# A fused attention and two-MLP kernel: attention rounds taken two at a time, a new order of its first 36 turns, copies along their target, and an earlier start of the weight fold

## The chip, the cores and the metric

One core of a Trainium2 chip runs the whole program. The metric is device time in microseconds (us). TensorE (PE in the profile) does the products, ScalarE (ACT), VectorE (DVE) and GpSimd (POOL) work on the data between them, and SyncE (SP) issues all transfers from its one queue, in order.

## The reference

The weights arrive as float64, q, k and v as float32; the output is float32.

```
# attention: B=4, H=8, S=576, D=64; heads 0-3 "plain", heads 4-7 "dilated"
scores = q @ k.T / sqrt(D)
plain:   keep 0 <= i-j < 32
dilated: keep 0 <= i-j < 128 and (i-j) % 4 == 0
attn = softmax(scores);  x = attn @ v      # as tokens: x is 2304 x 512
# MLP 1: 512 -> 2048 -> 512
x = leaky(x @ w_in, 0.01) @ w_out
# MLP 2: 512 -> 1024 (two branches) -> 1024 -> 512
out = ((x @ w1) * (x @ w2)) @ w3 @ w_out2
```

## The kernel before

**Precision.** A float64 weight is turned to float32 on the chip (`to_float32`, L145: one scaling and two reads of the raw tile, L151 and L153 always on ScalarE, a shift and an add on VectorE, L157), then split into a high and a low part (`split_steps`, L108). Every product of the MLPs is three matmuls (`mm3`, L117, lines L120 to L122).

**Attention** goes in 32 rounds: a batch has four pairs of heads (two dilated, two plain), and each pair two rounds of five or four blocks of 64 queries. A round n is: the scores `ps_s` (L394: 16 or 20 small matmuls of 96 columns), scaling and mask (VectorE), the maximum, the exponentials (ScalarE, one for each block, L418), a normalization (POOL), the transposes `ps_p` with their copies to `pT` (ScalarE), the values `ps_o` (L472: 16 or 20 small matmuls of 64 columns), and two copies of the result into `x`, high part on ScalarE (L500), low part on VectorE (L503). For the first batch q and k are transposed by TensorE into `ps_qT` and `ps_kT`, and one copy each (L374, the engine by `TURN_ON`) writes `qT` or `kT` of 576 columns. Later batches are transposed on VectorE (`turn_halves`, L273 and L286). Scores, values, and the transposes of later rounds share two PSUM banks ("side").

**MLP 1** goes in turns. The tokens are cut into seven chunks (columns 320, 256, 320, 256, 384, 384, 384); turn (c, f) is chunk c with hidden block f of 16. `hidden_steps` makes 12 matmuls into `ps_h` and an activation `g` (ScalarE, L563), whose split parts feed the 12 matmuls of `project_steps` (`ps_x`) two turns later. `ps_h` has two PSUM banks, which the transposes `ps_w3T` share.

**Order.** Attention of batches 0 and 1, the conversion of the 32 MLP 1 weight tiles (`MLP_CONV` names their engines) and the first 36 turns stand in an order written out by hand: each letter of `START` is one step of one stage; `LOADS` is the order of its loads, and `RAW_AT` and `PAIR_AT` say in which buffers conversions work. After it the loop over turns runs; at each turn `pace` moves on the generator `attention(16, 32)` for batches 2 and 3. A `ps_s` or `ps_o` block thus stands as a block of small matmuls between the long matmuls of the MLP.

**Fold.** w3 @ w_out2 is computed on the chip. From turn `LATE` on, when attention is done, `begin_fold` sets up 12 conversions (8 tiles of w_out2, whose finished parts `wo2` are also written to memory, then 4 of w3, each turned by four transposes `ps_w3T`, L672), with two buffers for raw tiles, `rawf`. Each turn adds `FOLD_PACE` steps; a step is one conversion (`rf` is written by its two ScalarE reads), and once nine are made the products `ps_wp` too:

```
            conv3.step()
            if conv3.made < NI + 1:      # NI = 8
                return
            while w3T:
                ...
                wp_step()
```

**Last stretch.** In chunk 6, w1 and w2 are converted, and the fold's result comes back by `load_wp` and `split_wp`; then come the gate products `ps_ab` and the output `ps_y`.

Of the kernel before, what the change touches and what calls it, by code (L numbers as in the profile page):

```python
# [28 lines left out]
def tile_window_attention_two_mlps(  # L29
# [70 lines left out]
    def copy_on(e):  # L100
        return e.copy if e is nc.scalar else e.tensor_copy
# [134 lines left out]
    nat_t, v_t, qk_t = {}, {}, {}  # L236


    order, seq = [], []
    for b in range(B):  # L240
        plain = [b * HP + i for i in range(HP // 2)]
        dilated = [b * HP + i for i in range(HP // 2, HP)]
        seq += dilated + plain
        order += [(pi, r) for pi in dilated for r in range(2)]
        order += [(pi, r) for r in range(2) for pi in plain]

    def pair(pi):
        b, h0 = divmod(pi, HP)
# [108 lines left out]
    def turn_rows(m):  # L357
        pi, nm = seq[m // 2], "qk"[m % 2]
        plain = pair(pi)[2]
        c = 6 if plain else 8  # L360
        n = S // c
        t = nat_t.pop((nm, pi))
        ps = bank2(f"ps_{nm}T{pi}")
        for g in range(2):
            for c1 in range(c // 2):
                src = t[:n, g * (c // 2) + c1].rearrange("p j d -> p (j d)")
                nc.tensor.transpose(ps[:, g, c1 * n : (c1 + 1) * n], src, ident[:n, :n])
        yield
        dst = att.tile([P, S], F32, tag=nm + "T", name=f"{nm}T{pi}", bufs=2)
        if plain:  # L370
            to = dst.rearrange("d (p g c) -> d g c p", g=2, p=n)
        else:
            to = dst.rearrange("d (c p g) -> d g c p", g=2, p=n)
        copy_on(engine_of[TURN_ON[m]])(to, ps[:, :, : S // 2].rearrange("d g (c p) -> d g c p", p=n))  # L374
        qk_t[nm, pi] = dst
        yield

# [81 lines left out]
    def value_steps(n):  # L459

        pi, r = order[n]
        b, hp = divmod(pi, HP)
        t = pt.pop(n)
        nb = t.shape[1]
        ps = side_bank(f"ps_o{n}")[:, : nb * QB]
        b, hp = divmod(pi, HP)
        plain = pair(pi)[2]
        vt = v_t[4 * b + 2 * plain + r]
        h = 2 * (hp % (HP // 2))
        for i in range(nb):  # L470
            for j in range(2):
                nc.tensor.matmul(  # L472
                    ps[j * D : (j + 1) * D, i * QB : (i + 1) * QB],
                    vt[i][:, h + j, :],
                    t[:, i, j * QB : (j + 1) * QB],
                    start=True, stop=True,
                )
        yield
        x = xs[hp][:, :, b % 2 * S : (b % 2 + 1) * S]
        views = []  # L480
        s0, s1 = r * HS[0], r * HS[0] + nb * QB
        if plain:
            views.append((x[:, :, s0:s1], ps))
        else:
            spans = []
            for g in range(DILATION):
                j0, j1 = max(0, s0 - g * SR), min(SR, s1 - g * SR)
                if spans and spans[-1][2:] == (j0, j1):
                    spans[-1] = (spans[-1][0], spans[-1][1] + 1, j0, j1)
                elif j0 < j1:  # L490
                    spans.append((g, 1, j0, j1))
            x = x.rearrange("d i (j r) -> d i r j", r=DILATION)
            for g, m, j0, j1 in spans:
                src = bass.AP(
                    ps.tensor, ps.offset + g * SR + j0 - s0,
                    [list(ps.ap[0]), [SR, m], [1, j1 - j0]],
                )
                views.append((x[:, :, g : g + m, j0:j1], src))
# [12 lines left out]
    def attention(n0, n1):  # L511

        for m in range(n0, n0 + 4):
            transpose_qk(m)
            load_qk(m + 2)
            if m % 2:
                yield
        load_v(n0 // 2 + 1)
        scores(n0)
        yield  # L520
        scores(n0 + 1)
        normalize(n0)
        yield
        for n in range(n0, n1):
            run(turn_p(n))
            normalize(n + 1)
            yield
            if n % 8 != 3:
                scores(n + 2)
                yield  # L530
            transpose_qk(n + 4)
            load_qk(n + 6)
            yield
            if n % 8 == 3:
                scores(n + 2)
                yield
            run(value_steps(n))
            m = n // NA * 4
            if n % NA in (2, 3):
                load_v(m + n % NA)  # L540
            elif n % NA in (5, 7):
                load_v(m + 4 + (n % NA == 7))
            yield


# [221 lines left out]
    with ExitStack():  # L767
# [39 lines left out]
        RAW_AT = "WWWWWWWWWWWWWWWWWWWWWWWWNWNWNWNW"  # L807
        PAIR_AT = "KKVVKKVVKKVVKKVVKKVVKKVKVKVKVKVK"

        def raw_early(i):  # L810
            place, tag, bufs = homes[RAW_AT[i]]
# [8 lines left out]
        for f in range(NF + AHEAD):  # L820
# [13 lines left out]
        runs += [(c, 0, NF) for c in range(2, NCH)]  # L834
        turns = [(c, f, f0, f1) for c, f0, f1 in runs for f in range(f0, f1)]
        START = (
            "L~L~~~~LTL~Y~~LT~Y~~TSYLTMLSXYEMSLX~M~~RETXN~YL~PERTLNSYCL~RVMNPXxSCyELTMLPYLVCXTxRE"
            "yVNLYL~PLxRSLGCLyNAL~MVGBXPxDLSEyUSMA~D~R~CX~N~MBVGEXLGPD~U~C~~RDxNVIyAOPx~GC~y~BHDI"
            "ULAOIVGgOHBcxGLEylHUgDIRDANgcBOPcAGJLCUBDlIVLUAOxBlHyGULADIHgOBcAJGLUgADlBHcIlLUBOHI"
            "LUgGOHIDAGOIJDBGOALUgJADGgBcDlALHUIZBOHILczGBOJgDLAGlJBcDlALUgHBcUIlLUJILOgIUGJOIDGA"  # L840
            "HOBDGALHUgLADOIcBHGOALclBGJglBDUADHIUBcUIlJgUIOgIHcGOlAGDJgOADBOJGcUBlHIcGAlOAHDGBZg"
            "DBUHgDLAULIUBHOIUzGIOJADGIOBJDALUGLcOBJclIDAOglJGcUgAlDIHcBGOALDBHUgGIUADHOBlILUBJOI"
            "UgOIJcOF|JcLlFgHcLlSlgSMLXJMEFJcXlELHRcNlHgRFLPgNJCLPclJCFVSxcLlyHFSgMLXHMEXVFSxRgyJ"
            "NEMFPcHZClzXSgRENVMHXLxRENyHgPRHNCPJCJclgVclJxLgyPclJCVclVxyJxyHclHgHgHgJJclgJclZczl"
            "JJclSSMXMEXRENPRNCVxyPCVxyLLL"
        )
        LOADS = "0123a45b67cwwdwwwwwwwwwwwwwwwwwwwwwwwwwwwwww89ABefCDEFghGHi"
        def late_turn(i):
            turn_halves(2 * HP + i)
            yield  # L850
# [108 lines left out]
        for c, f0, f1 in runs:  # L959
# [28 lines left out]
            for f in range(f0, f1):  # L988
# [77 lines left out]
```

## Time and profile before

| | |
|---|---|
| three timed runs | 866.89, 867.5, 869.97 us; median 867.5 |
| profiled execution | 868.56 us |
| its span | 866.6 us (1.96 us lie outside it) |
| granted TensorE clock, mean | 0.998 |
| TensorE busy | 848.2 us, 98% |
| ScalarE, VectorE, GpSimd busy | 352.6, 346.7, 210.8 us |
| DMA | 103.58 MB |

All times that follow are of the profiled execution, counted from the start of its span. A window's row gives each engine's busy time within the stretch; a wait is the idle time of an engine ahead of an instruction, with what ended it; matmuls are pipelined, so a matmul's own duration is longer than the distance to the next one's start.

### The profile page before, as it was taken

The page shows a single profiled execution, that of the slowest core. Times are in us where ns is not written, and L with a number is a line of the kernel's source. Part 1 is how long each engine was busy: PE and PEld are TensorE (multiplying, and loading weights), DVE is VectorE, ACT ScalarE, POOL GpSimd, SP SyncE. Part 2 cuts the span into 40 slices and gives each one's busy share as a digit, 9 for nine tenths or more (in the row PEclk, how much of TensorE's full clock was granted, in tenths as well). Part 3 has the DMA queues.
Part 4 walks back from the last instruction along what each step waited for, and adds up shares of the span by engine and source line. Part 5 has one row for each costly group of instructions (what it writes and reads, how often), then busy time and mean ns, then how long its engine had stood idle before and what let it go on. Part 6 is the DMA issues. An engine that isn't in the chain of part 4 may idle for free.

```text
span 866.6 us, 14693 instructions
## 1 busy us (share of the span) xinstructions
PE 848.2 (98%) x5774; PEld 772.0 (89%) x5774; DVE 346.7 (40%) x704; ACT 352.6 (41%) x879; POOL 210.8 (24%) x236
## 2 busy tenths in 40 slices
PE   7999998999999999999999999999999999999998
PEld 7799997999999999989899999998888888888887
DVE  4999976344453432274434177731021011000000
ACT  4999945223443343364433175632131121111111
POOL 3311101122322232263222134223123112111110
PEclk9999999999999999999999999999999999999999
DMA  6976575183333311189887575341001000000001
GB/s 152 309 214 231 179 169 137 34 193 73 82 98 92 78 45 50 47 294 349 300 289 236 165 239 155 113 135 49 25 1 61 24 13 13 25 12 13 25 13 48
DMA packets 87333, 103.58 MB, mean 120 GB/s; under 512 B 42849, under 2 KB 65633, under 8 KB 87265
## 3 DMA queue, kind: packets, MB, share of 16 engines
q1 hardware_dynamic: 87264, 102.65, 39.0%
q8 instruction: 45, 0.74, 0.4%
q14 instruction: 24, 0.19, 0.1%
HBM read 85.72 MB, written 16.91 MB: 118 GB/s over the span
## 4 chain that ended last, share of the span: by engine, by line
PE 77%; DMA 7%; DVE 6%; ACT 5%; issue 4%; POOL 2%; SPq 0%; POOLq 0%; DVEq 0%; ACTq 0%
PE ps_ab L120 7%; PE ps_ab L122 7%; PE ps_ab L121 7%; PE ps_x L120 6%; PE ps_x L122 5%; PE ps_x L121 5%; PE ps_h L120 5%; PE ps_h L122 5%; PE ps_h L121 5%; PE ps_y L122 4%; PE ps_y L121 4%; PE ps_y L120 4%; PE ps_s L394 2%; PE ps_o L472 2%; PE ps_wp L122 2%
## 5 line engine op out<-in xcount | busy, mean ns | idle before, releaser
L120 PE MATMUL ps_h<-x,win 128*128 128x384 f32 (+2 forms) x448 | 142.5, 318 | 4.9 <-ACT g L563 4.2
L122 PE MATMUL ps_h<-x,win 128*128 128x384 f32 (+2 forms) x448 | 140.7, 314 | 0.0
L121 PE MATMUL ps_h<-x,win 128*128 128x384 f32 (+2 forms) x448 | 140.4, 313 | 0.0
L120 PE MATMUL ps_x<-gs,wout 128*128 128x384 f32 (+2 forms) x368 | 119.0, 325 | 0.0
L743 DVE TENSOR_TENSOR ab<-a,ps_ab 128x512 f32<-128x512 f32 (+1 forms) x40 | 25.2, 633 | 233.3 <-ACT a L741 225.8
L120 PE MATMUL ps_ab<-ys,w 128*128 128x512 f32 (+1 forms) x320 | 117.7, 368 | 0.6 <-DVE ab L743 0.6
L121 PE MATMUL ps_x<-gs,wout 128*128 128x384 f32 (+2 forms) x368 | 117.7, 320 | 0.1
L122 PE MATMUL ps_ab<-ys,w 128*128 128x512 f32 (+1 forms) x320 | 117.7, 368 | 0.0
L121 PE MATMUL ps_ab<-ys,w 128*128 128x512 f32 (+1 forms) x320 | 117.6, 368 | 0.0
L122 PE MATMUL ps_x<-gs,wout 128*128 128x384 f32 (+2 forms) x368 | 117.4, 319 | 0.0
L112 POOL TENSOR_TENSOR p<-ab,p 128x512 fp32r<-128x512 f32 (+1 forms) x40 | 47.0, 1177 | 211.3 <-ACT p L110 211.3
L110 DVE CAST gs<-g 128x384 fp32r<-128x384 f32 (+2 forms) x92 | 41.3, 449 | 128.9 <-ACT g L563 103.3
L120 PEld LDWEIGHTS ps_h<-x,win 128*128 128x128 f32 x448 | 84.8, 189 | 8.2 <-ACT g L563 6.1
L112 POOL TENSOR_TENSOR gs<-g,gs 128x384 fp32r<-128x384 f32 (+2 forms) x64 | 59.5, 929 | 133.5 <-DVE gs L110 133.5
L563 ACT ACTIVATE g<-ps_h 128x384 f32<-128x384 f32 (+2 forms) x112 | 49.1, 439 | 96.8 <-PE ps_h L122 80.2
L121 PEld LDWEIGHTS ps_h<-x,win 128*128 128x128 f32 x448 | 84.9, 190 | 0.3
L122 PEld LDWEIGHTS ps_h<-x,win 128*128 128x128 f32 x448 | 84.8, 189 | 0.4
L741 ACT COPY a<-ps_ab 128x512 f32<-128x512 f32 (+1 forms) x40 | 21.6, 543 | 139.5 <-PE ps_ab L122 139.5
L120 PEld LDWEIGHTS ps_x<-gs,wout 128*128 128x128 f32 x368 | 69.5, 189 | 1.7
L121 PEld LDWEIGHTS ps_x<-gs,wout 128*128 128x128 f32 x368 | 69.7, 189 | 1.3 <-POOL gs L112 0.4
L122 PEld LDWEIGHTS ps_x<-gs,wout 128*128 128x128 f32 x368 | 69.7, 189 | 0.6
L120 PEld LDWEIGHTS ps_ab<-ys,w 128*128 128x128 f32 x320 | 60.1, 188 | 11.1 <-DVE ab L743 1.0
(109 smaller groups left out, 1553.1 us busy)
## 6 DMA issues: line engine op xcount, KB each, us to landing
wo<-wo_dram SPq DMA_DIRECT2D x32, 512.0 KB
raw<-in_moe_w_in_dram SPq DMA_DIRECT2D x16, 512.0 KB
raw<-in_moe_w_out_dram SPq DMA_DIRECT2D x16, 512.0 KB
rawf<-in_moe_w_dram SPq DMA_DIRECT2D x16, 512.0 KB
raww<-in_moe_w_dram SPq DMA_DIRECT2D x16, 512.0 KB
q<-in_q_dram SPq DMA_DIRECT2D x48, 140.0 KB
k<-in_k_dram SPq DMA_DIRECT2D x48, 140.0 KB
v<-in_v_dram SPq DMA_DIRECT2D x60, 96.0 KB
```

The lines of the kernel that those rows point to most:

```text
L110: copy_on(e_hi)(hi, src)
L112: e_lo.tensor_tensor(lo, src, hi.bitcast(F32), op=ALU.subtract)
L120: nc.tensor.matmul(ps, a[1], b[0], start=first, stop=False)
L121: nc.tensor.matmul(ps, a[0], b[1], start=False, stop=False)
L122: nc.tensor.matmul(ps, a[0], b[0], start=False, stop=last)
L394: nc.tensor.matmul(ps[j * QB : (j + 1) * QB, i - bl.start], qt[d, i * QB : (i + 1) * QB], kt[d, first_key(i, plain) : first_key(i, plain) ...
L472: nc.tensor.matmul(ps[j * D : (j + 1) * D, i * QB : (i + 1) * QB], vt[i][:, h + j, :], t[:, i, j * QB : (j + 1) * QB], start=True, stop=True,)
L563: nc.scalar.activation(g, ps, AF.Prelu, alpha=SLOPE)
L741: nc.scalar.copy(t, ps[0][:, :n])
L743: nc.vector.tensor_tensor(g, t, ps[1][:, :n], op=ALU.mult)
```

## The change

Attention takes two rounds at a time: both transposes, both values, both scores, both normalizations. Its steps go from 68 to 36, and `pace` is set to match. In batch 3 the plain heads come first, and `v_seq` orders the loads of v to suit. `START` is a new order: five warm-up matmuls (`~`) fewer, batch 1's attention spread otherwise among the turns; with it go `LOADS`, `RAW_AT`, `PAIR_AT`, `MLP_CONV` (GpSimd 10, VectorE 13, ScalarE 9 of the first scalings, against 14, 11, 7) and `TURN_ON` (five of eight copies on ScalarE, against two). The copies of `qT`, `kT` and of the dilated heads' `x` run through their target in order and step through PSUM. The fold begins after turn (4, 11) instead of (4, 13), takes 1.4 and later 1.3 steps a turn instead of 1.35, and stops at nine conversions until turn (5, 3). `wpf` has two buffers.

```diff
-    TURN_ON = "DDAADDDD"
-    MLP_CONV = tuple(x + "AD" for x in "GGDGGDGGADADGDGGAGGDDADADGGGAADD")
+    TURN_ON = "AAADADAD"
+    MLP_CONV = tuple(x + "AD" for x in "GGDGDDGGADAADAADDGADAGGADDDDGAGD")
...
+        if b == B - 1:
+            rounds, pairs, v_order = rounds[::-1], pairs[::-1], v_order[2:] + v_order[:2]
...
-            to = dst.rearrange("d (p g c) -> d g c p", g=2, p=n)
+            to, dims = dst.rearrange("d (p g c) -> d p g c", g=2, p=n), "d g (c p) -> d p g c"
...
-            x = x.rearrange("d i (j r) -> d i r j", r=DILATION)
-            for g, m, j0, j1 in spans:
+            x = x.rearrange("d i (j r) -> d i j r", r=DILATION)
+            edges = sorted({0, s0 % SR, s1 % SR, SR})
+            for j0, j1 in zip(edges, edges[1:]):
+                g = [g for g in range(DILATION) if s0 <= g * SR + j0 and g * SR + j1 <= s1]
                 src = bass.AP(
-                    ps.tensor, ps.offset + g * SR + j0 - s0,
-                    [list(ps.ap[0]), [SR, m], [1, j1 - j0]],
+                    ps.tensor, ps.offset + g[0] * SR + j0 - s0,
+                    [list(ps.ap[0]), [1, j1 - j0], [SR, len(g)]],
                 )
...
-        for n in range(n0, n1):
+        for n in range(n0, n1, 2):
             run(turn_p(n))
-            normalize(n + 1)
             yield
-            if n % 8 != 3:
-                scores(n + 2)
-                yield
-            transpose_qk(n + 4)
-            load_qk(n + 6)
+            run(turn_p(n + 1))
...
-            run(value_steps(n))
+            for i in (n, n + 1):
+                run(value_steps(i))
...
+            for i in (n + 2, n + 3):
+                scores(i)
...
+            for i in (n + 2, n + 3):
+                normalize(i)
             yield
...
-        t = late.tile([P, DM], F32, tag="wpf", name=f"wpf{ib}", bufs=1)
+        t = late.tile([P, DM], F32, tag="wpf", name=f"wpf{ib}", bufs=2)
...
-        LATE = (4, 13)
-        FOLD_PACE = 1.35
+        LATE, HOLD = (4, 11), (5, 3)
+        FOLD_PACE = (1.4, 1.3)
...
-                    owed[0] += FOLD_PACE
-                    while owed[0] >= 1:
+                    held = (c, f) < HOLD
+                    owed[0] += FOLD_PACE[not held]
+                    while owed[0] >= 1 and not (held and conv3.made > NI):
                         owed[0] -= 1
                         fold_step()
```

**TensorE in the loop over turns, an attention block.** Before, the scores of a round (here round 24; `x10` is ten rows of two matmuls) stand alone among the products `ps_x` of turn (3, 7), and so do the values of round 22, some 25 rows later:

```order
L451 MATMUL ps_p22_1_3569<-ident_84,s22_3330 96x128
L394 MATMUL ps_s24_3606<-kT14_3506,qT14_3367 64x96 x10
L121 MATMUL ps_x3_0_0_3277<-gs_1654,wout7_1266 128x256
...
L122 MATMUL ps_h3_10_3639<-x3_79,win10_1272 128x256
L472 MATMUL ps_o22_3665<-pT22_3571,v11_3272 64x64 x8
L120 MATMUL ps_x3_0_0_3277<-gs_1654,wout8_1289 128x256
```

In the changed kernel two rounds' blocks follow each other at once, here the scores of rounds 20 and 21 within the hidden products of turn (3, 4), and their values ahead of the products of turn (3, 6):

```order
L121 MATMUL ps_h3_4_3338<-x2_78,win4_888 128x256
L400 MATMUL ps_s20_3164<-kT8_2842,qT8_2835 64x96 x10
L400 MATMUL ps_s21_3186<-kT9_3062,qT9_3055 64x96 x10
L122 MATMUL ps_h3_4_3338<-x2_78,win4_888 128x256
...
L122 MATMUL ps_h3_8_3572<-x3_79,win8_1233 128x256
L478 MATMUL ps_o20_3354<-pT20_3251,v10_3125 64x64 x10
L478 MATMUL ps_o21_3367<-pT21_3323,v10_3125 64x64 x10
L120 MATMUL ps_x3_0_0_3286<-gs_1921,wout6_1257 128x256
```

In this part of the program scores make seven such pairs and values eight; before, scores and values shared a block in three places, and stood alone in the others.

**TensorE at the first transposes of w3.** Before, they stand one by one among the products of turn (5, 2), and hidden products of turns (5, 3) and (5, 4) are ahead of them:

```order
L122 MATMUL ps_x5_0_1_4885<-gs_1654,wout1_860 128x384
L672 MATMUL ps_w3T0_4964<-ident_84,wf8_4914 128x128 x4
L121 MATMUL ps_x5_0_0_4884<-gs_1654,wout2_937 128x384
```

In the changed kernel the products of turns up to (5, 3) come first, and then three transposed tiles and twelve products of the fold stand in one run ahead of the hidden products of turn (5, 4) (of the twelve rows of `ps_wp` the first and the last are shown):

```order
L122 MATMUL ps_x5_0_1_4893<-gs_1921,wout3_1009 128x384
L684 MATMUL ps_w3T0_4931<-ident_84,wf8_4843 128x128 x4
L684 MATMUL ps_w3T1_4954<-ident_84,wf9_4922 128x128 x4
L120 MATMUL ps_wp0_0_4962<-wo2_0_0_4939,w3T0_4936 128x512
...
L122 MATMUL ps_wp0_1_4963<-wo2_1_1_4941,w3T0_4936 128x512
L684 MATMUL ps_w3T2_4989<-ident_84,wf10_4945 128x128 x4
L120 MATMUL ps_h5_4_5025<-x0_76,win4_888 128x384
```

Between the last value matmuls (`ps_o31`) and `ps_w3T0` there were 181 long matmuls, and there are now 114.

**ScalarE in the same place.** Before, an activation `g` stands every few rows between the reads `rf` of a raw tile (`rf8` is the ninth conversion):

```order
L151 ACTIVATE rf8_4915<-rawf8_4865 128x512
L153 ACTIVATE rf8_4915<-rawf8_4865 128x512
L634 COPY st_86<-ps_x4_0_1_4085 128x384
L110 CAST wo2_7_4923<-wf7_4871 128x512
L563 ACTIVATE g_85<-ps_h5_3_4898 128x384
L563 ACTIVATE g_85<-ps_h5_4_4939 128x384
L151 ACTIVATE rf9_4956<-rawf9_4878 128x512
```

In the changed kernel the reads for conversions 5 to 12 and their splits stand between two activations; the first and the last rows of that run are

```order
L575 ACTIVATE g_85<-ps_h5_3_4906 128x384
L110 CAST wo2_3_4716<-wf3_4666 128x512
L151 ACTIVATE rf4_4708<-rawf4_4632 128x512
...
L110 CAST w3T1_4959<-ps_w3T1_4954 128x512
L151 ACTIVATE rf10_4946<-rawf10_4850 128x512
L153 ACTIVATE rf10_4946<-rawf10_4850 128x512
L151 ACTIVATE rf11_4981<-rawf11_4929 128x512
L153 ACTIVATE rf11_4981<-rawf11_4929 128x512
L110 CAST w3T2_4994<-ps_w3T2_4989 128x512
L575 ACTIVATE g_85<-ps_h5_4_5025 128x384
```

On ScalarE the reads of the 12 conversions stood between the activations of turns (4, 13) and (5, 5); they now stand between those of (4, 15) and (5, 4), eight of the twelve behind that of (5, 3).

## Rows read from the trace of the kernel before

**Rows 1.** The profile page: the span, and TensorE (PE): busy time, share, instructions.

```profile
span 866.6 us, 14693 instructions
...
PE 848.2 (98%) x5774; PEld 772.0 (89%) x5774; DVE 346.7 (40%) x704; ACT 352.6 (41%) x879; POOL 210.8 (24%) x236
```

**Rows 2.** Windows of two stretches (columns: stretch, length, busy time by engine, clock, DMA, GB/s).

```profile
60.00:80.00 20.00, 20.00 (x158) 20.00 (x157) 18.35 (x41) 19.56 (x36) 5.29 (x5) 1.00 0.89 299
112.00:166.00 54.00, 50.46 (x526) 47.45 (x526) 33.20 (x83) 22.55 (x91) 5.62 (x6) 1.00 0.49 120
```

**Rows 3.** Waits of TensorE, 112 to 166 us: total, times, longest.

```profile
PE ps_s L394 <- DVE kT L286: 0.9, 1, 0.9
PE ps_s L394 <- DVE x L503: 0.8, 1, 0.8
PE ps_h L120 <- ACT g L563: 0.7, 1, 0.7
```

**Rows 4.** The chain that ended last, whole span: start, us, what.

```profile
6.51 1.38 PE warm L884 x6
...
156.90 1.32 PE ps_o L472 x40
177.81 1.47 PE ps_s L394 x32
```

**Rows 5.** The same chain within 320 to 332 us.

```profile
328.59 0.81 PE ps_s L394 x16
329.40 0.37 PE ps_h L120
...
330.30 0.73 PE ps_o L472 x20
```

**Rows 6.** Groups by form, ScalarE (ACT), 0 to 166 us: busy, mean ns, idle before.

```profile
L500 ACT CAST x<-ps_o 128x288 fp32r<-128x288 f32 x4 | 2.7, 673 | 4.2 <-PE ps_o L472 4.2
...
L500 ACT CAST x<-ps_o 128x320 fp32r<-128x320 f32 x4 | 1.7, 424 | 1.7 <-PE ps_o L472 1.7
...
L374 ACT COPY kT<-ps_kT 128x576 f32<-128x576 f32 x1 | 0.7, 697 | 0.9 <-PE ps_kT L367 0.9
```

**Rows 7.** Timeline of ScalarE in the fold: start, us, instruction [idle before <-releaser].

```profile
359.69 0.37 ACT L500 CAST x<-ps_o 128x256 fp32r<-128x256 f32 x1 [3.03 <-PE ps_o L472]
...
361.89 0.78 ACT L151 ACTIVATE rf<-rawf 128x512 f16<-128x512 f32 x1
...
389.02 0.80 ACT L151 ACTIVATE rf<-rawf 128x512 f16<-128x512 f32 x1 [2.06 <-DMA rawf<-in_moe_w_dram]
...
395.74 0.81 ACT L151 ACTIVATE rf<-rawf 128x512 f16<-128x512 f32 x1 [2.75 <-DMA rawf<-in_moe_w_dram]
...
398.49 0.81 ACT L151 ACTIVATE rf<-rawf 128x512 f16<-128x512 f32 x1 [0.88 <-DMA rawf<-in_moe_w_dram]
```

**Rows 8.** Timeline of TensorE in the same stretch.

```profile
359.31 0.34 PE L472 MATMUL ps_o<-pT,v 96*64 96x64 f32 x4
...
384.26 0.45 PE L120 MATMUL ps_h<-x,win 128*128 128x384 f32 x1 [2.05 <-ACT g L563]
...
385.51 0.52 PE L120 MATMUL ps_h<-x,win 128*128 128x384 f32 x1
385.83 0.52 PE L121 MATMUL ps_h<-x,win 128*128 128x384 f32 x1
...
395.01 0.60 PE L672 MATMUL ps_w3T<-ident,wf 128*128 128x128 f32 x4
```

**Rows 9.** Windows within the fold, columns as in Rows 2.

```profile
362.00:380.00 18.00, 18.00 (x106) 18.00 (x105) 13.00 (x18) 12.23 (x20) 11.00 (x12) 1.00 0.69 244
384.00:388.00 4.00, 3.73 (x14) 3.74 (x15) 3.86 (x7) 2.89 (x6) 2.75 (x3) 0.67 0.68 200
...
396.00:400.00 4.00, 3.88 (x23) 3.52 (x22) 2.70 (x4) 3.06 (x5) 3.37 (x4) 1.00 1.04 418
```

**Rows 10.** Waits of TensorE, 500 to 600 us.

```profile
PE ps_h L120 <- ACT g L563: 1.2, 3, 0.6
```

More of the change, by code (lines that the diff above doesn't have):

```diff
@@ L236, in tile_window_attention_two_mlps @@
     nat_t, v_t, qk_t = {}, {}, {}
-    order, seq = [], []
+    order, seq, v_seq = [], [], []
     for b in range(B):
@@ L242, in tile_window_attention_two_mlps @@
         dilated = [b * HP + i for i in range(HP // 2, HP)]
-        seq += dilated + plain
-        order += [(pi, r) for pi in dilated for r in range(2)]
-        order += [(pi, r) for r in range(2) for pi in plain]
+        rounds = [(pi, r) for pi in dilated for r in range(2)]
+        rounds = [rounds, [(pi, r) for r in range(2) for pi in plain]]
+        pairs, v_order = [dilated, plain], [4 * b, 4 * b + 1, 4 * b + 2, 4 * b + 3]
+        if b == B - 1:
+            rounds, pairs, v_order = rounds[::-1], pairs[::-1], v_order[2:] + v_order[:2]
+        order += rounds[0] + rounds[1]
+        seq += pairs[0] + pairs[1]
+        v_seq += v_order
     def pair(pi):
@@ L321, in load_v @@
             return
+        m = v_seq[m]
         b, plain, r = m // 4, m % 4 >= 2, m % 2
@@ L370, in turn_rows @@
         if plain:
-            to = dst.rearrange("d (p g c) -> d g c p", g=2, p=n)
+            to, dims = dst.rearrange("d (p g c) -> d p g c", g=2, p=n), "d g (c p) -> d p g c"
         else:
-            to = dst.rearrange("d (c p g) -> d g c p", g=2, p=n)
-        copy_on(engine_of[TURN_ON[m]])(to, ps[:, :, : S // 2].rearrange("d g (c p) -> d g c p", p=n))
+            to, dims = dst.rearrange("d (c p g) -> d c p g", g=2, p=n), "d g (c p) -> d c p g"
+        copy_on(engine_of[TURN_ON[m]])(to, ps[:, :, : S // 2].rearrange(dims, p=n))
         qk_t[nm, pi] = dst
@@ L484, in value_steps @@
         else:
[L485 to L491, printed above, removed]
-            x = x.rearrange("d i (j r) -> d i r j", r=DILATION)
-            for g, m, j0, j1 in spans:
+            x = x.rearrange("d i (j r) -> d i j r", r=DILATION)
+            edges = sorted({0, s0 % SR, s1 % SR, SR})
+            for j0, j1 in zip(edges, edges[1:]):
+                g = [g for g in range(DILATION) if s0 <= g * SR + j0 and g * SR + j1 <= s1]
                 src = bass.AP(
-                    ps.tensor, ps.offset + g * SR + j0 - s0,
-                    [list(ps.ap[0]), [SR, m], [1, j1 - j0]],
+                    ps.tensor, ps.offset + g[0] * SR + j0 - s0,
+                    [list(ps.ap[0]), [1, j1 - j0], [SR, len(g)]],
                 )
-                views.append((x[:, :, g : g + m, j0:j1], src))
+                views.append((x[:, :, j0:j1, g[0] : g[-1] + 1], src))
         for x, src in views:
@@ L518, in attention @@
         load_v(n0 // 2 + 1)
-        scores(n0)
+        for n in (n0, n0 + 1):
+            scores(n)
         yield
-        scores(n0 + 1)
-        normalize(n0)
+        for n in (n0, n0 + 1):
+            normalize(n)
         yield
-        for n in range(n0, n1):
+        for n in range(n0, n1, 2):
             run(turn_p(n))
-            normalize(n + 1)
             yield
-            if n % 8 != 3:
-                scores(n + 2)
-                yield
-            transpose_qk(n + 4)
-            load_qk(n + 6)
+            run(turn_p(n + 1))
+            turn = [lambda m=m: (transpose_qk(m), load_qk(m + 2)) for m in (n + 4, n + 5)]
+            last = n >= (B - 1) * NA
+            late = n % NA == (0 if last else 4)
+            if not late:
+                for f in turn:
+                    f()
             yield
-            if n % 8 == 3:
-                scores(n + 2)
-                yield
-            run(value_steps(n))
+            for i in (n, n + 1):
+                run(value_steps(i))
             m = n // NA * 4
[L539 to L542, printed above, removed]
+            if last and n % NA in (0, 2):
+                load_v(m + 2 + n % NA // 2)
+            elif n % NA == 2:
+                load_v(m + 2)
+                load_v(m + 3)
+            elif n % NA in (4, 6):
+                load_v(m + 2 + n % NA // 2)
+            yield
+            for i in (n + 2, n + 3):
+                scores(i)
+            if late:
+                for f in turn:
+                    f()
+            for i in (n + 2, n + 3):
+                normalize(i)
             yield
@@ L806, in tile_window_attention_two_mlps @@
         }
-        RAW_AT = "WWWWWWWWWWWWWWWWWWWWWWWWNWNWNWNW"
-        PAIR_AT = "KKVVKKVVKKVVKKVVKKVVKKVKVKVKVKVK"
+        RAW_AT = "WWWWWWWWWWWWWWWWWNWNWNWWNNWNWWWW"
+        PAIR_AT = "VVKVKVKNVKKVKKVKKVKKVKKVKKVKKVKK"
         def raw_early(i):
@@ L836, in tile_window_attention_two_mlps @@
         START = (
[L837 to L845, printed above, removed]
+            "L~L~~~~LTL~Y~~LT~Y~~SLTMXSYLETMXL~Y~~RESNTMLRPXYNSCLETMXPLYVLCRSENMTxXVYLRPxyNLETyL~"
+            "Y~G~CSRDALNPMLBVLXCLSUxLEPMLGyVXSDxR~CG~N~yIMVEOPXF~C~~xVAGy~x~RA~yNBHGADLUBDIULBLDO"
+            "IgUHEOLcGAlHGgRADNIDgOAPcBJGClLUALDIPcVClOxVByLHxUByIUBHOIUgGOHIFLgLAJLgDLBOGJcGDlAL"
+            "cDLlBHcUALlIUHBOIUGSOIDSAGOJgADFGgHBZLALcBUHgDIUzHlIMgOBJXGOEDJGcUAlHRgcNMIBXHlAUgOB"
+            "HDIGEUDJOIRGAOJBNAcUJGcDIlDAJlOgBcGHglLBULADLUIHcBOIlLgUJGOgDAGJIcDBlAOHZGBUzLHADLUg"
+            "IclBJOgUIGOJIcGADlBDJcAOUBGJIcLDAULOBPlILHUClIGOAHDgGBOADHUgGBcIULPAJOClgDIFLJBLOLJU"
+            "cIFVcGLlHOxADGyBlLSDgUASMIJcBXFEHULGIRDANJMgXBOEUPLHOIRlCNJgOcF|HlFHgclcSglSMXHMEXVV"
+            "gRxHLENyJgRxNyJclPZHCczlPgHCVgVxLyHxyPJCVclHxgyHJJclgHclgJJclgHclHgJJclgJclZczlJJclS"
+            "SMXMEXRENPRCNVxyPCVxyLLL"
         )
-        LOADS = "0123a45b67cwwdwwwwwwwwwwwwwwwwwwwwwwwwwwwwww89ABefCDEFghGHi"
+        LOADS = "0123a45b67wcww8wwwwwwwwdww9ewwwAwwwwwwwwwwwwwBCwwDEwFfghGHi"
         def late_turn(i):
@@ L949, in pace @@
         def pace(c):
-            owed[0] += 39 / 28 if c < LATE[0] else 2.25
+            owed[0] += 26 / 28 if c < LATE[0] else 10 / 6
             while owed[0] >= 1:
```

## The prediction

> **What bounds the kernel now.** I read the profile page first. TensorE is busy for 848.2 of 866.6 us [rows 1], so most of what the change can win lies in 18 us of idle time and in matmuls that take longer than they must. Two views then say where. The windows show a stretch near the start where TensorE has no gap while ScalarE (19.56 of 20) and VectorE (18.35) have nearly none either, and a later one, 112 to 166 us, where TensorE idles for 54.00 - 50.46 = 3.5 us, the largest of it for a `kT`, an `x` and a `g` [rows 2, 3]. From there to the end TensorE waits little; the one wait over 2 us stands inside the fold [rows 8]. The chain of waits shows what no idle time shows: a block of small attention matmuls costs the long matmuls around it something at its edge. The long matmul behind a `ps_s` block takes 0.37 us in the chain [rows 5], against 0.17 us where long ones follow each other (106 in 18.00 us, [rows 9]).
>
> **The change, part by part.** The sum is made against the profiled execution, 868.56 us (span 866.6 and 1.96 outside it); the median of three, 867.5, lies 1.06 below it.
>
> *Rounds in pairs, loop over turns.* Two `ps_s` blocks of 16 cost 2 x 0.81 = 1.62 us apart, and 1.47 together; two `ps_o` blocks of 20 cost 1.46 apart and 1.32 together [rows 4, 5]. With the slower matmul behind the block (0.37 - 0.17 = 0.20) a pairing saves 0.15 + 0.20 or 0.14 + 0.20, so about 0.35 us of TensorE. Seven pairs of scores and eight of values make 15 x 0.35 = 5.25; three places shared a block already and a part of their 0.2 is gone, less 0.6: **-4.65**, from -3.5 to -5.5. This time is TensorE's own and nothing covers it, unless a wait on one of the two side banks takes it back (the fourth rival).
>
> *START.* A series of six warm-up matmuls takes 1.38 us in the chain [rows 4], so five are 5 x 0.23 = 1.15: **-1.2**. The chain `ident`, masks, first load of q decides there, so this may be nothing. Batch 1's attention is brought forward and spread, so that its `kT`, `x` and `g` are wanted at other times: of the 3.5 us [rows 2, 3] I let one wait of 1.0 stay, **-2.5** (0 to -3.5). Four more pairings by the price above: **-1.4**. The early part, to about 60 us, I put at nothing, from -2 to +3: ScalarE gets three more copies of 0.70 us [rows 6] and two more first scalings of 0.8 us (priced as the read of a raw tile, [rows 7]), 3.7 us in all, in front of the stretch where it is full, and VectorE and GpSimd lose as many. Together **-5.1**, from +3 to -9.
>
> *Copies along the target.* ScalarE's copy of 288 columns into a strided target takes 673 ns, one of 320 columns into a plain one 424 [rows 6]. If the target was what costs, each falls by some 0.25 us, 1.0 us for four; if a strided read of PSUM costs as much, nothing is won. No row shows such a read. Either way these copies lie beside matmuls, and I count 0. [...]
>
> *Second `wpf` buffer, chunk 6.* TensorE waits there 1.2 us in three waits [rows 10], behind activations that stand after the splits of w1, w2 and the fold's result on ScalarE. A buffer frees only the part that waits for the transfer: **-0.9**, from 0 to -1.2.
>
> *Fold.* Here the order shows what the diff alone does not. Call T the time of the last value matmul. Before, T is 359.31, the first read of a raw tile starts 2.6 us later, the ninth, which `ps_w3T0` needs, at 389.02, and the eleventh, which `ps_w3T2` needs, at 398.49 [rows 7, 8]: 27.1 and 36.6 us after the first. TensorE reaches `ps_w3T0` at 395.01 without a wait [rows 8], because 181 long matmuls (30.8 us), a wait and a slow stretch lie between. Now 114 lie between, 114 x 0.17 = 19.4 us, and after 3.8 us more (two sets of transposes, twelve products of 512 columns) `ps_w3T2`, so TensorE asks for the eleventh conversion at T + 23.2. The order starts the conversions little earlier against T: two copies of `x` stand ahead of them, T + 1.3.
> How long eleven conversions take decides. *Upper end:* the pace of before, 36.6 us, and about 2.2 from the reading to the finished tile: T + 40.1, a wait of **16.9 us**. *Lower end:* the transfers in the queue up to the eleventh raw tile (raw tiles, finished parts written and two read back, evacuated `x`) are 9.7 MB, of which 244 GB/s was the mean early in the fold and 418 the best 4 us [rows 9]. At 418 that is 23.2 us; with the longest wait of a read for its raw tile, 2.75 [rows 7], and the 2.2: T + 29.5, a wait of **6.3**. I take 13.5, nearer the upper end: there are still two raw buffers, and even at the slower pace of before reads waited 2.06, 2.75 and 0.88 us for their tile [rows 7], so what limited the late conversions was the transfer and not the turns. The burst only removes the activations between. Behind the waiting `ps_w3T` stand `ps_h` of (5, 4) and everything else of TensorE, so nothing hides the wait.
> [...] **13.5 + 1.5 - 3.6 = +11.4**, from 6.3 + 1.5 - 3.6 = +4.2 to +14.8.
>
> *Sum:* -4.65 - 5.1 - 0.9 + 11.4 = +0.75, so 869.3 us against the profiled 868.56, and less 1.06 **868.2 us** against the median.
>
> **The rivals.**
> *The fold keeps up* (0.19). If loads and conversions had waited for turns and not for transfers, packing them removes the stall: with 4 us of wait left the fold costs 4 + 1.5 - 3.6 = +1.9, and the time is 868.2 - 9.5 = 858.7. For it: only the last conversions waited on transfers, and much of 362 to 380 ran at 244 GB/s, below what the queue has shown [rows 9]. Against it: 9.7 MB in 23.2 us wants 418 GB/s throughout, the rate of the best 4 us.
> *START wins twice as much* (0.15): all of the 3.5 us and some 4 more before 60 us, -10: 868.2 - 4.9 = 863.3.
> *ScalarE sets the pace of the start, slower* (0.20). At 60 to 80 us it has 0.44 us to spare in 20 [rows 2]. If the 3.7 us that it gains are not outweighed, activations `g` come late and TensorE waits for them; with the copies' relief of 1.0 that is +2.7, the waits of rows 3 stay in another place, and START becomes -1.2 - 1.4 + 2.7 = +0.1: 873.4. It decides once ScalarE has more than about half a microsecond added in that stretch. [...]
> *Pairing saves nothing* (0.05): the second block of a pair waits for its side bank, which VectorE or ScalarE still empties, as long as it saves: 868.2 + 4.65 = 872.9. Against it: no wait of TensorE for a side bank is over 0.9 us in the rows of before [rows 3].
> *The forecast* has 0.41. [...]
>
> **How the numbers follow.** 0.5% (4.3 us: 863.2 to 871.8) is about what a measurement of this kernel can tell from no change. Faster: the first rival, two thirds of the second (its own spread is a few us) and a little of the forecast's lower side, 0.19 + 0.10 + 0.03 = 0.32. Slower: 0.20 + 0.05, less what of them stays under the bound, 0.24. The rest, 0.44, is no difference. The range takes in the fold at a wait of 2 to 3 us below and ScalarE's rival up to a START of +2 instead of -5.1 (its bound is +3): 857 to 875. The likeliest case alone, with the fold between 10 and 16 us of wait, runs from 864.7 to 870.7.
>
> **What would show it.** In the trace of after, between `ps_o31` and `ps_h5_4`: a wait of `ps_w3T` of 6 to 17 us, ended by VectorE's `wf`, with reads of `rawf` waiting for DMA ahead of it, and a clock below 1 behind it. In the chain: `ps_s` and `ps_o` in blocks of 32 to 40, 15 fewer slow matmuls. At 60 to 80 us: ScalarE near 20 of 20, with no wait for `g`. At 112 to 166 us: some 1 us of idle time instead of 3.5. The prediction is wrong if the `ps_w3T` wait is under 4 us (then the transfers were not what limited), or if waits for `g` above 2 us appear before 110 us.

## The result

The changed kernel takes 877.2 us (median of four runs, 876.0 to 878.1), the kernel before 867.6: a ratio of 1.011, interval 1.0093 to 1.0127. It is slower by 9.6 us, above the forecast of 868.2 and above its range.

The profile after, first the page (busy times, and the tenths of TensorE and of its granted clock in 40 slices of the span):

```profile
span 876.3 us, 14654 instructions
...
PE 845.0 (96%) x5764; PEld 774.2 (88%) x5764; DVE 338.0 (39%) x703; ACT 352.0 (40%) x884; POOL 204.0 (23%) x232
...
PE   8799999999999999984999999999999999999998
...
PEclk9999999999999999996999999999999999999999
```

TensorE is busy for 3 us less than in [rows 1], and the span is 9.7 us longer. One place stands out in both rows of tenths, in the nineteenth slice, 394 to 416 us. The waits of TensorE in the whole span (total, times, longest):

```profile
PE ps_w3T L684 <- DVE wf L157: 15.7, 3, 12.6
PE ps_h L120 <- DVE win L112: 2.2, 1, 2.2
PE ps_o L478 <- DVE x L504: 2.0, 1, 2.0
...
PE ps_p L457 <- POOL s L441: 1.4, 1, 1.4
PE ps_s L400 <- DVE s L415: 1.4, 1, 1.4
```

The first row did not exist before: 15.7 us of waits for the transposes of w3. It is the stall that the prediction placed there, at 13.5. The next rows, though, stand before 60 us and at 112 to 166 us, in the start, which the prediction had made 5.1 us faster.

To place the 9.7 us, take the starts of the first matmul of a turn's hidden products (turn n is the n-th group of twelve `ps_h` in the trace; START ends with turn 35, chunk 4 begins with turn 64, chunk 6 with turn 96):

```
start, us           turn 0   turn 36   turn 78   turn 96   turn 111   span
before                38.7     171.0     363.3     491.3      559.1    866.6
after                 40.2     173.1     358.5     506.5      568.9    876.3
length of stretch            to 36    36-78    78-96    96-111
before                       171.0    192.3    128.0      67.7
after                        173.1    185.4    148.0      62.4
difference                    +2.1     -6.9    +20.0      -5.3
```

The stretches are not term for term those of the prediction, since work moved between them. Of the -6.9 some 2.1 are transposes and values of the last two rounds, which before stood ahead of turn 78 and now stand behind it; and the fold's products now end two turns earlier, which lengthens 78 to 96 and shortens the rest. The three stretches behind turn 36 together give +7.8, and the start +2.1.

**The fold.** The timeline of TensorE after (start, duration, matmul, idle time before it and its releaser) answers to [rows 8]:

```profile
368.96 1.27 PE L478 MATMUL ps_o<-pT,v 96*64 96x64 f32 x36
...
402.75 1.12 PE L684 MATMUL ps_w3T<-ident,wf 128*128 128x128 f32 x4 [12.56 <-DVE wf L157]
405.77 1.11 PE L684 MATMUL ps_w3T<-ident,wf 128*128 128x128 f32 x4 [1.90 <-DVE wf L157]
...
408.39 0.63 PE L121 MATMUL ps_wp<-wo,w3T 128*128 128x512 f32 x1
408.82 0.63 PE L122 MATMUL ps_wp<-wo,w3T 128*128 128x512 f32 x1
...
412.70 0.63 PE L684 MATMUL ps_w3T<-ident,wf 128*128 128x128 f32 x4 [1.22 <-DVE wf L157]
```

The last values (the block of 36 that starts at 368.96) are followed by the products that the order promised, and then TensorE stands for 12.56 us, does four transposes, stands 1.90, and later 1.22. Behind the first wait the products of 512 columns start every 0.43 us. The windows of the same place say what else happened (columns as in [rows 9]):

```profile
368.00:372.00 4.00, 4.00 (x52) 3.68 (x52) 1.30 (x5) 2.19 (x7) 1.19 (x2) 1.00 0.00 0
384.00:388.00 4.00, 4.00 (x25) 4.00 (x24) 0.98 (x3) 2.04 (x3) 2.56 (x3) 1.00 0.95 343
392.00:396.00 4.00, 0.00 (x0) 0.00 (x0) 1.12 (x2) 1.94 (x3) 2.13 (x3) 0.71 0.97 359
400.00:404.00 4.00, 1.12 (x4) 0.72 (x4) 1.12 (x2) 1.81 (x3) 0.99 (x2) 0.50 0.98 339
404.00:408.00 4.00, 2.23 (x8) 1.94 (x9) 2.18 (x4) 2.00 (x4) 0.30 (x1) 0.50 1.04 408
```

From 390.2 us on TensorE had nothing, and the granted clock, 1.00 until 393.5, stood at 0.50 from 394.0 to 410.5 us (windows of 0.5 us). So the restart was paid for over nine products and eight transposes, where the trace of before has ten slow products (385.51 to 388.39 us, two of them in [rows 8]). DMA, idle at 368 to 372, carried 159 to 281 GB/s until 384, and from there 338 to 408 but for 198 at 396 to 400: 291 in the mean from the first read of a raw tile to that of the eleventh, where the prediction's lower end had 418. The chain that ends in the third `ps_w3T` (start, length, what) shows why that was not enough:

```profile
369.81 0.92 ACT x L501 x4
370.72 0.68 ACT rf L151
...
373.37 3.80 DMA rawf<-in_moe_w_out_dram
...
388.35 5.31 DMA rawf<-in_moe_w_out_dram
...
395.21 5.27 DMA rawf<-in_moe_w_dram
...
402.04 7.81 DMA rawf<-in_moe_w_dram
...
411.39 1.18 DVE wf L157
```

Right behind the last copies of `x` the reads `rf` begin, 0.5 us after the values end (368.96 + 1.27 = 370.23), and from there four loads of `rawf` stand in the chain, 3.80 + 5.31 + 5.27 + 7.81 = 22.2 us of the 42.8 between 369.8 and 412.6. With two raw buffers a load can only be issued when the reads before it are done (the chain goes from the reads straight into the load); that it is then slowed by the finished parts that are written beside it is argued, not shown.

The packed order did not make the conversions faster. In this trace the ninth raw tile is read 30.0 us after the first and the eleventh 39.3, against 27.1 and 36.6 before [rows 7]. In all eleven traces with rounds in pairs, whatever the fold's timetable, these distances are 28.7 to 31.3 and 37.7 to 40.1 us.

**The start.** The prediction put its early part at nothing. The timeline of TensorE after has two waits there, and a slow stretch behind the second (granted clock 0.69 at 44 to 48 us, with 0.50 from 45.5 to 48.5, as from 35.5 to 38.5 behind the first; 320 columns every 0.27 us, of which two of thirteen are shown, against 0.15 where the clock stands at 1.00):

```profile
35.07 1.22 PE L478 MATMUL ps_o<-pT,v 96*64 96x64 f32 x20 [2.04 <-DVE x L504]
...
44.39 0.39 PE L120 MATMUL ps_h<-x,win 128*128 128x320 f32 x1 [2.23 <-DVE win L112]
...
46.00 0.47 PE L120 MATMUL ps_h<-x,win 128*128 128x320 f32 x1
46.27 0.47 PE L121 MATMUL ps_h<-x,win 128*128 128x320 f32 x1
```

The first wait is one of VectorE's queue. Its timeline:

```profile
33.98 0.43 DVE L107 TENSOR_SCALAR pair<-raw 128x512 f32<-128x512 f32 x1 [1.74 <-DMA raw<-in_moe_w_in_dram]
34.32 0.50 DVE L504 TENSOR_TENSOR x<-ps_o,x 128x32 fp32r<-128x32 f32 x2
```

VectorE stands 1.74 us for a raw weight tile, and the low part of `x`, for which `ps_o` waits, is queued behind that conversion. The chain in this stretch goes on into the transfer of that tile:

```profile
25.84 8.11 DMA raw<-in_moe_w_in_dram
...
34.32 0.51 DVE x L504 x2
```

The new order of loads has put a load of q for batch 1 right behind the third raw tile, and the tile took 8.1 us to land (early_raw, below, moves that load).

The loss is there in every profiled execution. From turn 0 to turn 8 the six traces with the start of before take 23.7 to 23.8 us, the five with the new one as it stands 27.9 to 30.2. Some 2.1 us of that are 36 score matmuls and 4 transposes that the new order has in this stretch (priced by such blocks at 351 to 365 us); the other 2.0 to 4.3 are lost. Behind turn 17 a part comes back: 76.5 to 81.4 us to turn 36, against 79.7 to 82.5, with 36 score matmuls fewer.

**The copies.** The groups of ScalarE and VectorE by form (busy, mean ns, idle before), beside [rows 6]:

```profile
L501 ACT CAST x<-ps_o 128x224 fp32r<-128x224 f32 x8 | 2.9, 368 | 0.0
...
L501 ACT CAST x<-ps_o 128x256 fp32r<-128x256 f32 x2 | 0.7, 374 | 0.0
L380 ACT COPY kT<-ps_kT 128x576 f32<-128x576 f32 x1 | 0.6, 639 | 1.7 <-PE ps_kT L373 1.7
```

```profile
L380 DVE COPY kT<-ps_kT 128x576 f32<-128x576 f32 x3 | 2.3, 751 | 0.2 <-PE ps_kT L373 0.2
```

The larger round's `x` copy on ScalarE was 673 ns for 288 columns and 267 for 32; now it is 368 for 224 and 241 for 96, 0.33 us less. `kT` on ScalarE went from 697 to 639, and on VectorE to 751; the same copy with the strided target took 1044 there, in old_copies below:

```profile
L380 DVE COPY kT<-ps_kT 128x576 f32<-128x576 f32 x3 | 3.1, 1044 | 2.2 <-PE ps_kT L373 2.2
```

In these copies, on either engine, reading PSUM with a stride into a target in order cost less than reading in order into a strided target (`kT`: 639 ns against 697 on ScalarE, 751 against 1044 on VectorE). The prediction had left open whether it would cost as much.

### The profile page after: what moved, and what is told of

Same layout as the page of the kernel before. It is cut to its first block, busy times and chain, and to the rows that moved or that the text cites. A ratio compares the mean times of both kernels' runs of the same rounds, so it can differ in the third digit from the quotient of the medians.

```text
span 876.3 us, 14654 instructions
## 1 busy us (share of the span) xinstructions
PE 845.0 (96%) x5764; PEld 774.2 (88%) x5764; DVE 338.0 (39%) x703; ACT 352.0 (40%) x884; POOL 204.0 (23%) x232
## 4 chain that ended last, share of the span: by engine, by line
PE 84%; DMA 6%; SPq 3%; ACT 2%; DVE 2%; POOL 1%; issue 1%; ACTq 0%; DVEq 0%; POOLq 0%
PE ps_ab L120 7%; PE ps_ab L122 7%; PE ps_ab L121 7%; PE ps_h L120 7%; PE ps_h L122 7%; PE ps_h L121 7%; PE ps_x L120 7%; PE ps_x L121 7%; PE ps_x L122 7%; PE ps_y L120 4%; PE ps_y L122 4%; PE ps_y L121 4%; PE ps_s L400 2%; PE ps_o L478 2%; PE ps_wp L122 2%; PE ps_wp L121 2%
## 5 line engine op out<-in xcount | busy, mean ns | idle before, releaser
L121 PE MATMUL ps_x<-gs,wout 128*128 128x384 f32 (+2 forms) x356 | 112.9, 317 | 0.0
L122 PE MATMUL ps_x<-gs,wout 128*128 128x384 f32 (+2 forms) x356 | 112.8, 317 | 0.0
L120 PE MATMUL ps_x<-gs,wout 128*128 128x384 f32 (+2 forms) x356 | 112.7, 319 | 0.0
L575 ACT ACTIVATE g<-ps_h 128x384 f32<-128x384 f32 (+2 forms) x112 | 49.1, 438 | 90.0 <-PE ps_h L122 71.1
L110 DVE CAST gs<-g 128x384 fp32r<-128x384 f32 (+2 forms) x89 | 33.6, 377 | 123.1 <-ACT g L575 101.6
L120 PEld LDWEIGHTS ps_ab<-ys,w 128*128 128x128 f32 x320 | 60.0, 188 | 10.6 <-DVE ab L755 0.6
L121 PEld LDWEIGHTS ps_ab<-ys,w 128*128 128x128 f32 x320 | 60.2, 188 | 10.1
L122 PEld LDWEIGHTS ps_ab<-ys,w 128*128 128x128 f32 x320 | 60.1, 188 | 10.0
L120 PEld LDWEIGHTS ps_x<-gs,wout 128*128 128x128 f32 x356 | 67.0, 189 | 0.8
```

What stands on the lines that cost most here:

```text
L110: copy_on(e_hi)(hi, src)
L120: nc.tensor.matmul(ps, a[1], b[0], start=first, stop=False)
L121: nc.tensor.matmul(ps, a[0], b[1], start=False, stop=False)
L122: nc.tensor.matmul(ps, a[0], b[0], start=False, stop=last)
L575: nc.scalar.activation(g, ps, AF.Prelu, alpha=SLOPE)
```

## The experiments

Times are medians; each is compared with the kernel before on the same chip (867.6 to 868.3 us there).

**fold_before.** The fold's timetable of before in the changed kernel:

```diff
-        LATE, HOLD = (4, 11), (5, 3)
-        FOLD_PACE = (1.4, 1.3)
+        LATE, HOLD = (4, 13), (0, 0)
+        FOLD_PACE = (1.35, 1.35)
```

> The changed kernel with the fold's timetable of before (LATE (4, 13), 1.35 steps a turn, no hold); all else as changed. Theory A, the packed conversions with the early ps_w3T cost some 15 us (15.7 of waits and a half clock behind them): about 862 us, no wait of ps_w3T over 3 us. Theory B, the paired attention ends too late (its last values at turn (5, 0) instead of (4, 12)) and leaves the fold too little time whatever its timetable: a wait of 8 us or more stays at ps_w3T, and the time is 870 or more.

Measured: 873.9 us, ratio 1.0065 (1.0031 to 1.0098). The waits in 360 to 500 us:

```profile
PE ps_w3T L684 <- DVE wf L157: 12.5, 1, 12.5
```

Theory A fell and theory B holds: the wait stays above 8 us and the time above 870. Without hold and burst two of the three waits go, and 3.2 us with them; the large one stays as it was. In the order the last values still stand at turn (5, 0), and 19.7 us of products lie between them and `ps_w3T0`, exactly as in the changed kernel.

**start_before.** The changed kernel with START, LOADS, RAW_AT, PAIR_AT, TURN_ON and MLP_CONV of before (strings only, as in the diff above, reversed).

> The changed kernel with the hand-written start of before (START, LOADS, RAW_AT, PAIR_AT, TURN_ON, MLP_CONV); all else as changed, the fold's stall too. Theory A, the new start loses some 5 us before 60 us (a raw tile that comes late, half clock behind two waits) and gives back some 3 behind 112 us: 877.2 - 2.1 = 875.1, with the fourth turn's first product near 50 us instead of 54. Theory B, the loss before 60 us comes from the copies along their target or from code outside the start: it stays at 877 or more, with that product at 53 to 54 us.

Measured: 874.95 us, ratio 1.0071 (1.0046 to 1.0096); turn 3 begins at 49.1 us, turn 36 at 170.1. That is what theory A had, 2.3 us under the changed kernel, though the two were timed on different occasions and the runs spread from 872.3 to 876.5.

**both_before.** Both edits together.

> Start and fold timetable of before, with the rounds in pairs, the copies along their target and the second wpf buffer. Theory A: pairs -5.0 and chunk 6 -2.2 against before, so 867.6 - 7.2 = 860.4. Theory B, the pairing's gain in the loop over turns belongs to the new start (other rounds are left over for the loop): 865 or more.

Measured: 873.7 us, ratio 1.0068 (1.0048 to 1.0089); theory A missed by 13 us, since the fold's wait is there (11.3 us in one piece). The time lies in theory B's range, but not for its reason. The loop itself keeps its gain: turns 36 to 78 take 185.4 us, as in every kernel of this study with rounds in pairs, and 192.3 in both with single rounds. So that gain does not come from START. Against fold_before, timed on the same occasion, the start of before wins 0.1 us here.

**wpf2.** The kernel before with one edit:

```diff
-        t = late.tile([P, DM], F32, tag="wpf", name=f"wpf{ib}", bufs=1)
+        t = late.tile([P, DM], F32, tag="wpf", name=f"wpf{ib}", bufs=2)
```

> The kernel before with two wpf buffers, nothing else. Theory A, the single buffer holds the splits of the fold's result on ScalarE and so the activations of chunk 6: 867.6 - 2.2 = 865.4, no wait for an activation g between 500 and 600 us. Theory B, the waits in chunk 6 come from the conversions of w1 and w2 queued there: 867 to 868, the three waits of 1.2 us in sum stay.

Measured: 865.7 us, ratio 0.9973 (0.9954 to 0.9992), and the waits for `g` of [rows 10] are gone; one row is left in 500 to 600 us:

```profile
PE ps_ab L120 <- DVE ab L743: 0.6, 1, 0.6
```

Theory A holds: -2.0 us (by the interval -0.7 to -4.0), and the buffer held all three waits and not a part of them.

**late_fold.** The changed kernel with a fold that begins later:

```diff
-        LATE, HOLD = (4, 11), (5, 3)
-        FOLD_PACE = (1.4, 1.3)
+        LATE, HOLD = (4, 15), (0, 0)
+        FOLD_PACE = (1.35, 1.35)
```

> The changed kernel with the fold begun after turn (4, 15), 1.35 steps a turn, no hold: the last values stay at turn (5, 0), but 32 us of products lie between them and the first ps_w3T (19.7 us in the changed kernel and in the one with the fold's timetable of before). Theory B as it stands now, the distance from the last values to the first ps_w3T decides, and the paired attention had shortened it: the ps_w3T wait falls under 3 us, the half clock behind it goes, and the time is 877.2 - 15 = 862. Theory C, the slow part is the fold's own work (raw tiles through two buffers beside the stores), wherever it stands: some 8 us of waits come back at later transposes, and the time is 870 or more.

Measured: 860.7 us, ratio 0.9925 (0.9904 to 0.9946), and 861.1 us, 0.9906 (0.9889 to 0.9923), when run again. All waits in 360 to 500 us, and the first transposes:

```profile
PE ps_x L121 <- POOL gs L112: 0.5, 1, 0.5
PE ps_w3T L684 <- DVE wf L157: 0.2, 1, 0.2
```

```profile
404.66 0.66 PE L684 MATMUL ps_w3T<-ident,wf 128*128 128x128 f32 x4
...
407.39 0.66 PE L684 MATMUL ps_w3T<-ident,wf 128*128 128x128 f32 x4
```

The wait is 0.2 us in place of 15.7. Against fold_before the edit is one number, LATE, two turns later, and it is worth 13.2 us. The last values are still at (5, 0); the distance from them to `ps_w3T0` grew, from 114 long matmuls (19.7 us) to 186 (32.2 us). The reads wait for their tiles as before (a load of 6.0 and one of 7.1 us stand in the chain of the fold), but TensorE no longer waits for the reads. Theory C fell: nothing came back at later transposes.

**late_fold_start.** The same with the start of before.

> The same late fold with the start of before. If the start's loss and the fold's stall are independent: 862 - 2.5 = 859.5, that is 8 us under the kernel before (pairs -6, chunk 6 -2). If the loop's gain is given back at later transposes (theory C): 866 or more.

Measured: 861.3 us, ratio 0.9938 (0.9921 to 0.9954). The loop's gain stays, but against late_fold the start of before wins nothing here (it is 0.6 us slower), while against the changed kernel it had won 2.3.

**old_copies.** late_fold_start with the two copy forms of before (the lines of the diff on `to` and `views`, reversed).

> The kernel with late fold and start of before, and with the copies of before (strided target, PSUM read in order). Theory A, the copies lie beside matmuls: the time of late_fold_start within 1 us, though each copy gets 0.1 to 0.3 us longer. Rival, ScalarE and VectorE set the pace of the start and the longer copies delay the first products: 1.5 to 3 us slower than late_fold_start.

Measured: 862.1 us, ratio 0.9938 (0.9923 to 0.9953), 0.8 us over late_fold_start with intervals that overlap: theory A. The kernel differs from wpf2 by the pairs (with batch 3's order) and the later fold alone: 865.7 - 862.1 = 3.6 us are theirs, across two occasions.

**early_raw.** The changed kernel, the load of q moved back:

```diff
-        LOADS = "0123a45b67wcww8wwwwwwwwdww9ewww...
+        LOADS = "0123a45b67wcwwwwwwwwwwdww89ewww...
```

and the step `F` that transposes it set beside the next `F`.

> The changed kernel with one load of q for batch 1 (and its transpose on VectorE) moved back behind the raw weight tiles of the first eleven loads, to where the load of k stands; the fold's stall stays. Theory A, that load and its descriptors delay the raw tile on which VectorE's queue stops at 34 us, and with it ps_o and the fourth turn's win: the waits of 2.0 and 2.2 us and the half clock go, the first product of turn 3 falls from 54 to 50 or 51 us and the time to 873.5 to 874.5. Theory B, the loss comes from the order of the steps themselves (ScalarE and VectorE get other work first): turn 3 stays at 53 or more and the time at 876 to 878.

Measured: 881.5 us, ratio 1.0162 (1.0145 to 1.0179). Neither theory holds. Turn 0 came at 36.1 us and turn 3 at 50.1, four earlier, as theory A has it, though the wait for `win` stayed (2.3 us); turn 8 came at 73.9, four later. The waits of TensorE, and VectorE's timeline ahead of the new one:

```profile
PE ps_w3T L684 <- DVE wf L157: 15.7, 3, 13.7
PE ps_x L120 <- DVE wout L112: 6.2, 1, 6.2
```

```profile
54.52 1.68 DVE L291 STREAM_TRANSPOSE qT<-q 128x160 f32<-128x160 f32 x4 [0.46 <-DMA q<-in_q_dram]
60.70 1.60 DVE L291 STREAM_TRANSPOSE kT<-k 128x160 f32<-128x160 f32 x4 [4.50 <-DMA k<-in_k_dram]
62.15 0.40 DVE L141 TENSOR_SCALAR pair<-pair 128x512 int32<-128x512 int32 x1
62.48 0.66 DVE L112 TENSOR_TENSOR wout<-pair,wout 128x512 fp32r<-128x512 f32 x1
```

The load of k behind it needed a buffer that the transpose of q gives back; so it was issued only at 56.2 us, where that transpose ends, VectorE stood 4.50 us for it, and the `wout` for which TensorE waited is two rows behind in VectorE's queue.

**early_raw2.** late_fold with a milder form of it (the load behind five raw tiles, its `F` 34 steps later):

> late_fold with the first load of q for batch 1 moved back behind five raw weight tiles only, and its transpose on VectorE 34 steps of the start later, but still ahead of the load of k, which in early_raw had to wait for it (VectorE then stood 4.5 us before that k, and TensorE 6.2 us before a wout). Theory A, what the new start loses before 55 us is the raw tiles behind that load: the first product of turn 0 comes 3 to 4 us earlier, that of turn 8 no later than in late_fold, and the time falls by 2 to 4 us, to 857 or 858. Theory B, the raw tiles come earlier but VectorE and ScalarE are full from 40 to 110 us, so that the lead is lost again by turn 17: 860 to 862.

Measured: 864.7 us, ratio 0.9953 (0.9935 to 0.997), 3.6 us over late_fold_again. Turn 0 starts at 36.2 us, 2.1 earlier; turn 17 at 96.9, 2.8 later. TensorE waits in other places:

```profile
PE ps_h L120 <- DVE win L112: 2.3, 1, 2.3
...
PE ps_h L120 <- ACT wout L110: 2.0, 1, 2.0
```

Theory A fell: the raw tile holds the first products, but their lead is lost again, as theory B has it. The time is above theory B's range too, and the lead is gone by turn 3 already (53.9 us against 51.4 in late_fold_again), with the granted clock at 0.74 in 40 to 60 us around the two waits. At 80 to 112 us VectorE and ScalarE are busy for 31.3 and 31.5 of 32 us in this run too. That the making of weight tiles is the limit there is argued from this, not shown by a run of its own.

**fold50.** late_fold with LATE (5, 0) and 1.5 steps a turn:

> late_fold with the fold begun one turn later still, after (5, 0), 1.5 steps a turn: the first ps_w3T is as far behind the last values (32 us of products), the second comes right behind it. If only the distance to the transposes matters: 860 to 861 with a wait of at most 2 us at the second transposes. If the pace of conversions matters too (3.4 us for each by the trace, 2.8 are given): 863 or more.

Measured: 865.7 us, ratio 0.9963 (0.9942 to 0.9984), runs from 862.2 to 872.7. Not conclusive. The waits at the transposes are 2.0 us, as the first reading has it, and turns 78 to 96 take 130.7 us (131.0 in late_fold_again). But turns 96 to 111 take 67.7 us against 64.9: both stretches together are 2.5 us longer, with TensorE idle for 4.4 us in place of 1.7, which speaks for the second reading (the pace matters too), as the median does. And this execution had lost most of its time in the start already (turn 36 at 179.7 us, 170.6 in late_fold_again), with the same START.

**late_fold_again** is quoted with late_fold:

> The same kernel as late_fold, as the base of the next two on the same chip: 860 to 861 us.

## Why the prediction was wrong

*Rounds in pairs, -4.65.* Right. Turns 36 to 78 became 6.9 us shorter, of which some 2.1 is work that moved behind turn 78: -4.8. The rival that a side bank takes it back has no row: TensorE does not wait at all in these turns. The timed pair gives 3.6 (wpf2 against old_copies), the later fold included.

*Start, -5.1.* This step failed: "The early part, to about 60 us, I put at nothing", with gains everywhere else. In the two traces START cost +2.1 us. The executions of the new start reach turn 36 at 170.6 to 179.7 us in five profiles, those of the old one at 169.0 to 173.3 in six; in the timed pairs the new one costs 2.3 us (changed kernel against start_before) or 0.1 (fold_before against both_before), or wins 0.6 (late_fold against late_fold_start). Nothing of the 5.1 came in any of them. The late part did what was forecast: the idle time at 112 to 168 us is 1.4 us, one wait, in place of 3.5. The early part ate it (2.0 to 4.3 us between turns 0 and 8): the sum priced ScalarE's instructions and left out SyncE's queue and the raw tiles, on which VectorE stood. The rival that ScalarE sets the pace came nearer in size (+0.1) but had another place: ScalarE is busy for 18.1 of 20 us at 60 to 80 us, and no wait for `g` over 0.2 us stands before 110 us. The range stated for START does not follow at its lower end: the lowest values of its terms add up to -8.1, not -9.

*Second wpf buffer, -0.9.* The kind was right, the size too small: -2.0 by wpf2, whose interval just takes in -0.9; turns 96 to 111 went from 67.7 to 66.0 us in the traces. The prediction let the buffer free only a part of the three waits for `g`; all three went with it.

*Fold, +11.4.* The mechanism and the place were right (three waits at `ps_w3T`, reads waiting for DMA ahead of them, a granted clock of 0.50 behind), and the size was near the upper bound: 15.7 us of waits against 13.5, of a range of 6.3 to 16.9. No run shows the 1.5 us that the sum has for the restart behind this wait. The trace of before shows 1.5 us behind its wait of 2.05: ten matmuls of 384 columns that follow each other by 0.32 us in place of 0.17 [rows 8], with the granted clock at 0.50 from 385.5 to 388.5 us; 2.05 + 1.5 is the 3.6 that the sum takes off, as that wait was for an activation `g` [rows 8]. Behind the fold's wait the clock was at 0.50 from 394.0 to 410.5 us: nine products with some 0.2 us more each and two sets of transposes with 0.45 make about 2.7. And the conversions took longer than the upper end allowed, 39.3 us from the first read to the eleventh in place of 36.6. From the stretches, 78 to 111 is 14.7 us longer; with the work that moved in (-2.1) and the second wpf buffer (+2.0) the fold's own term is about +14.6. What decides is what the prediction counted, the distance between the last values and the first transposes (19.4 us there, 19.7 measured). What it did not say is where the shorter distance came from. The burst and the earlier start of the fold are not the reason: fold_before has neither, and still waits 12.5 us. Attention ends at turn (5, 0) instead of (4, 13), since pairs put a turn between each stage of a pair, and a fold that is timed from the turn number does not move with it. late_fold moves it, and the wait is gone. That the pairing and not the new `pace` set with it makes attention end later is read from the order; no run separates them. Nor did a run try a third raw buffer.

Together -4.8 + 2.1 - 2.0 + 14.6 = +9.9, against a difference of the spans of 9.7. The start's term stands in that sum as its stretch measured, so the agreement is no test of it. The prediction's sum was +0.75: 7.2 us of the gap are the start and 3.2 the fold, with 1.1 given back by wpf.

*The version that beats both* is late_fold, 860.7 and 861.1 us, 0.8 to 0.9% under the kernel before: pairs, the second wpf buffer, and a fold two turns later instead of two earlier.

*Left open:* what the new start costs in all, and which wait makes its early turns slow. Executions of one START differ by 9 us at turn 36 (170.6 in late_fold_again, 179.7 in fold50), more than the two starts do in the mean, and both attempts to mend the loads made another wait.

## What to carry to other kernels

Where a stage is timed by a counter of the loop and fed by one that ends by its own pace, look in the order at the distance between the last instruction of the one and the first of the other, in microseconds of work of the engine that must not wait, and compare it with the length of the chain that has to fit in. A stall found so can be cured by moving the later stage back, even if "earlier" looked like the gain. And a reordered start is priced on every queue, the one that issues transfers first: here a tile that took 8.1 us to land stopped what stood behind its conversion in VectorE's queue, a copy of attention that TensorE was waiting for.

## What the runs showed of the hardware that was not expected

Copies of 224 columns that step through PSUM by 144 words and write two neighbours at a time took 368 ns on ScalarE, where a plain copy of 256 took 374. With a strided target 288 columns had taken 673, where a plain copy of 320 took 424 [rows 6].

After a wait of 12.6 us, four transposes and a second wait of 1.9 us, the granted clock stood at 0.50 for nine products more, until 410.5 us, some 8 us from the first transposes on; behind the 2.05 us wait of before it stood at 0.50 for three microseconds, 385.5 to 388.5 us, and at 1.00 from 389 on.
